# A single-token attention and MLP block: wq's load split into 16 and 112 rows

## The chip, the cores and the metric

The kernel runs on one core of one Trainium2 chip. Each core has five engines: TensorE (PE, matmuls and weight loads), VectorE (DVE), ScalarE (ACT), GpSimd (POOL) and SyncE (SP), and here SP issues nearly all of the loads. 16 DMA engines move the bytes from HBM to SBUF, the memory with 128 partitions from which the engines compute. The metric is the device time of one execution in microseconds; the time before is the median of three runs.

## The reference: what is computed

One token x of 512 values goes through a pre-norm block. Attention reads a cache of 32768 keys and values for each of 32 heads of width 128, and an MLP with a mish activation follows:

```python
q = (layernorm(x) @ wq) per head                 # wq 512 x 4096
p = softmax(q . k_cache * 128**-0.5)             # k_cache 32 x 32768 x 128, bf16
h = x + (p @ v_cache) @ wo                       # v_cache as k_cache, wo 4096 x 512
z = layernorm(h) @ w1 + b1                       # w1 512 x 1376
out = h + (z * tanh(softplus(z))) @ w2           # w2 1376 x 512
```

Each head has 8.39 MB of keys and as much of values. With one query there is one use for each byte that is loaded.

## The kernel before

SBUF holds a ring of six slots of 32 KB a partition (L354, `ring`). Two pairs of slots take the keys of even and odd heads in turn, one pair takes values; the weights lie in the same slots before and after (`HOMES`, L470). wq, 4 MB, is put into the first slot of the value pair: 128 partitions, 32 KB in each. Row p of the load holds rows 4p to 4p+3 of the matrix, so that it is one contiguous run of 32 KB in HBM.

`order` (L456 to L459) is the order in which SP issues loads: wq, the keys of head 0, and then for each head the next keys and the values before; at the end wo, the last values and the MLP's weights. wq itself is issued ahead of the Block that holds the engines' programs (L882). The SP program then starts with the two loads of the bias b1 (L563 and L564, behind a wait for GpSimd's zeroing of their tile), and goes on to the keys (L590). `start` (L550) issues a load on SP that raises a semaphore by 16 when it has landed. The keys of head 0 are cut into three loads and those of head 1 into two; all other key loads but the last are whole. The first values wait for wq's slot to be free (`freed_by`, L497).

Meanwhile x is loaded on ACT's queue (L601), turned by PE, and normalized (L623 to L639) into xnT. PE then makes all queries at once (L642 to L648): 128 matmuls, each with a 128 x 128 block of wq as weights, the first of which waits for xnT and for wq's semaphore. `ready_wait` (L484) gives that semaphore: `ready` of the slot, at 16 times the number of the fill, and wq is that slot's first fill. The last of these matmuls frees wq's slot.

For each head PE turns the keys, 128 x 128 at a time (L690), VectorE copies the turned keys out of PSUM (L696), and PE multiplies them with the query (L666). The softmax follows (L730 to L753), and PE multiplies the values with the weights (L717). PE's program is a loop over heads, as is VectorE's. The end is the projection by wo, the second layernorm, and the MLP (L788 to L872).

Of the kernel before, what the change touches and what calls it, by code (L numbers as in the profile page):

```python
# [291 lines left out]
def bass_sequential_preLN__mha_block_cached__dense_activation_mish__decode_kernel(  # L292
    nc: bass.Bass,
    A_x: bass.AP,
    A_k_cache: bass.AP,
    A_v_cache: bass.AP,
    A_wq: bass.AP,
    A_wo: bass.AP,
    B_x: bass.AP,
    B_w1: bass.AP,  # L300
    B_b1: bass.AP,
    B_w2: bass.AP,
    out: bass.AP,
):
    build_kernel(nc, A_x, A_k_cache, A_v_cache, A_wq, A_wo, B_w1, B_b1, B_w2, out)


def build_kernel(nc, A_x, A_k_cache, A_v_cache, A_wq, A_wo, B_w1, B_b1, B_w2, out):
# [6 lines left out]
    KC = D // 128  # L315
# [26 lines left out]
    def sb(shape, dt, name):  # L342
        cm = nc.sbuf_tensor(name, shape, dt)
        t = cm.__enter__()
        allocs.append(cm)
        return t.ap()
# [7 lines left out]
    ring = sb([128, NS, SLOT], BF16, "ring")  # L354
# [53 lines left out]
    sem = nc.alloc_semaphore  # L408
# [3 lines left out]
    ready = [sem(f"ready{i}") for i in range(NS)]  # L412
    sems["keys_in"] = (ready[0], ready[HALVES])
    s_x = sem("s_x")
    s_b1 = sem("s_b1")
    s_out = sem("s_out")
    WQ, WO, WL = ("wq",), ("wo",), ("wl",)
# [54 lines left out]
    def slot_of(what):  # L472
        if what in HOMES:
            return HOMES[what]
        if what[0] in ("w1", "w2"):
            return HOMES[WL]
        return V_HOME if what[0] == "v" else what[1] % 2 * HALVES
# [6 lines left out]
    def ready_wait(what):  # L484
        if what == WL:
            return (s_wl, 16)
        return (ready[slot_of(what)], 16 * fills[what])

    def free_name(what):
        return "free" + "_".join(map(str, what))  # L490
# [50 lines left out]
    def program(S):  # L541
# [13 lines left out]
        for what in order:  # L555
# [13 lines left out]
            elif what[0] == "w1":  # L569
                k = what[1]  # L570
                start(w1_v[:, k, :], B_w1[k * 128:(k + 1) * 128, :], w1_sems[k])
            elif what[0] == "w2":
                n = what[1]
# [6 lines left out]
            else:  # L580
                kind, h = what
# [14 lines left out]
              waits=["fin"])  # L596
# [45 lines left out]
        for h in range(H):  # L642
            for kc in range(KC):
                last = h == H - 1 and kc == KC - 1
                S.step(PE, lambda h=h, kc=kc: t_.matmul(Q_REG[:, h:h + 1], wq_v[:, kc, h * Dh:(h + 1) * Dh],  # L645
                                                         xnT[:, 0, kc:kc + 1], start=(kc == 0), stop=(kc == KC - 1)),
                       name=(["q", free_name(("wq",))] if last else None),
                       waits=(["xn0", ready_wait(("wq",))] if h == 0 and kc == 0 else ()))  # L648
        S.step(DVE, lambda: v.tensor_copy(qT[:, 0:H], Q_REG), name="qT", waits=["q"])  # L649
        S.step(DVE, lambda: v.tensor_copy(qcur[:, :], qT[:, 0:1]), name="qc0", waits=["qT", "qTz", "oTz"], kind="qc")  # L650

# [227 lines left out]
    log = {}  # L879
    counted = _Sched(nc, False, events, sems, log)  # L880
    program(counted)
    nc.sync.dma_start(ring[:, slot_of(WQ), :], A_wq.rearrange("(p k) n -> p (k n)", k=KC)).then_inc(ready[slot_of(WQ)], 16)  # L882
    with nc.Block() as block:
        for eng_name, attr in ((POOL, "gpsimd"), (SP, "sync"), (DVE, "vector"), (ACT, "scalar"), (PE, "tensor")):
            emitter = _Sched(nc, True, events, sems, log, only=eng_name)

            def _run(eng, emitter=emitter):
                program(emitter)
            getattr(block, attr)(_run)
            assert emitter.cnt == counted.cnt  # L890
# [31 lines left out]
```

## Time and profile before

| | |
|---|---|
| three runs | 1275.12, 1275.36, 1275.61 us; median 1275.36 |
| span of the profiled execution | 1273.1 us (its own device time isn't listed beside it) |
| PE busy | 1019.9 us, 80% |
| DVE busy | 718.2 us, 56% |
| bytes moved | 548.22 MB, mean 431 GB/s |
| mean granted TensorE clock | 0.766 |
| issue of wq | starts at 0.75 us, takes 0.39 us |

The span goes from the first to the last instruction of one execution. A busy share is an average over the whole span, and PE's includes time in which it works at a lower granted clock. The DMA share of a window is the mean busy share of the 16 DMA engines; a packet's bytes and time are booked where it starts, so that in short windows the share can exceed 1. A row of waits gives the engine and line that waited, on what, and how long in total, how often, and the longest.

### The profile page before, as it was taken

To read this page: it belongs to the slowest core of one execution; us is meant where nothing else is said; L and a number is where in the kernel's file an instruction comes from. 1 tells how busy PE (TensorE), PEld (TensorE's weight loads), DVE (VectorE), ACT (ScalarE), POOL (GpSimd) and SP (SyncE) were. 2 spreads that over 40 slices of the span, in tenths; PEclk is the share of its full clock that TensorE was granted. 3 is DMA by queue.
4 is the path that set the end of the run, shared out by engine and by line. 5 is a ranking of instruction groups with operands and counts; after the bars stand their busy time and mean duration, and the time that the engine had idled before them with its cause. 6 is when DMAs were issued, how large, how long until landed. Compare 5 with 4: busy or idle time off the path is not lost.

```text
span 1273.1 us, 54451 instructions
## 1 busy us (share of the span) xinstructions
PE 1019.9 (80%) x25046; PEld 993.3 (78%) x25047; DVE 718.2 (56%) x1257; ACT 20.6 (2%) x71; POOL 0.9 (0%) x7
## 2 busy tenths in 40 slices
PE   4789877779777789777798777797777897777996
PEld 4789877779777779777788777797777887777994
DVE  3656664456654456644566544566545666444661
ACT  0000000000000000000000000000000000000000
POOL 0000000000000000000000000000000000000000
PEclk9778877678877778776788777788767887777885
DMA  9999999999999999999999999999999999999998
GB/s 406 442 417 438 432 439 432 432 434 430 432 441 428 437 434 428 432 439 432 434 434 430 430 439 434 430 434 434 428 434 441 428 437 432 430 432 439 427 427 360
DMA packets 12214, 548.22 MB, mean 431 GB/s; under 512 B 1348, under 2 KB 1454, under 8 KB 2862
## 3 DMA queue, kind: packets, MB, share of 16 engines
q1 hardware_dynamic: 12204, 548.09, 99.7%
q8 instruction: 8, 0.13, 0.0%
q10 hardware_dynamic: 2, 0.00, 0.0%
HBM read 548.09 MB, written 0.00 MB: 431 GB/s over the span
## 4 chain that ended last, share of the span: by engine, by line
DMA 54%; DVE 23%; PE 19%; issue 2%; SPq 2%; POOL 0%; POOLq 0%
DMA ring<-in_A_k_cache_dram 51%; DVE ering L696 23%; PE ops L717 9%; PE tps L690 7%; DMA ring<-in_A_v_cache_dram 2%; SPq L551 2%; PE sps L666 1%; DMA ring<-in_B_w_dram 1%; PE hlp L741 1%; PE hlp L736 1%; PE hlp L751 0%; PE tps L867 0%; DVE pmax L730 0%; DVE perm L872 0%; DVE gmax L738 0%
## 5 line engine op out<-in xcount | busy, mean ns | idle before, releaser
L690 PE MATMUL tps<-identb,ring 128*128 128x128 bf16 x8192 | 671.7, 233 | 208.8 <-DMA ring<-in_A_k_cache_dram 203.2
L696 DVE COPY ering<-tps 128x1024 bf16<-128x1024 bf16 x1024 | 669.7, 691 | 261.6 <-PE tps L690 261.1
L690 PEld LDWEIGHTS tps<-identb,ring 128*128 x8192 | 525.4, 105 | 211.6 <-issue 211.6
L666 PE MATMUL sps<-qcur,ering 128*128 128x1 bf16 x8192 | 343.7, 164 | 7.3 <-DVE ering L696 6.6
L666 PEld LDWEIGHTS sps<-qcur,ering 128*128 128x128 bf16 x8192 | 309.4, 97 | 10.1 <-DVE ering L696 9.4
L717 PEld LDWEIGHTS ops<-pbuf,ring 128*128 128x128 bf16 x8192 | 226.4, 103 | 23.3 <-issue 15.1
L717 PE MATMUL ops<-pbuf,ring 128*128 128x1 bf16 x8192 | 231.3, 165 | 10.6 <-DMA ring<-in_A_v_cache_dram 7.2
L725 DVE TENSOR_TENSOR oT<-ops,rtotc 128x1 f32 x31 | 5.0, 161 | 110.6 <-PE ops L717 110.6
L738 DVE TENSOR_REDUCE gmax<-hlp 1x1 f32<-1x128 f32 x32 | 8.9, 279 | 64.5 <-PE hlp L736 64.5
L743 DVE TENSOR_SCALAR nbias<-hlp 128x1 f32<-128x1 f32 x32 | 5.1, 158 | 63.5 <-PE hlp L741 63.5
L746 ACT ACTIVATE pbuf<-sps,nbias 128x256 bf16<-128x256 f32 x32 | 15.2, 474 | 1219.7 <-PE ops L717 1166.8
L730 DVE TENSOR_REDUCE pmax<-sps 128x1 f32<-128x256 f32 x32 | 13.6, 424 | 14.3 <-PE sps L666 14.3
L736 PE MATMUL hlp<-ident,pmax 128*1 128x128 f32 x64 | 17.1, 363 | 2.5 <-issue 2.5
L741 PE MATMUL hlp<-gmax,onesmat 1*128 1x1 f32 x64 | 18.5, 356 | 0.4 <-DVE gmax L738 0.4
L741 PEld LDWEIGHTS hlp<-gmax,onesmat 1*128 1x128 f32 x64 | 15.8, 304 | 1.3 <-DVE gmax L738 0.9
L751 PE MATMUL hlp<-esum,onesmat 128*128 128x1 f32 x64 | 12.1, 259 | 4.7 <-issue 0.6
L751 PEld LDWEIGHTS hlp<-esum,onesmat 128*128 128x128 f32 x64 | 9.8, 191 | 7.1 <-issue 7.1
L645 PE MATMUL hlp<-xnT,ring 128*128 128x1 bf16 x128 | 3.6, 165 | 9.2 <-DMA ring<-in_A_wq_dram 9.2
L645 PEld LDWEIGHTS hlp<-xnT,ring 128*128 128x128 bf16 x128 | 3.5, 104 | 9.3 <-issue 9.3
L725 DVE TENSOR_TENSOR oL<-ops,rtotc 128x1 bf16<-128x1 f32 x1 | 0.2, 161 | 12.4 <-PE ops L717 12.4
L649 DVE CAST qT<-hlp 128x32 bf16<-128x32 f32 x1 | 0.2, 192 | 11.5 <-PE hlp L645 11.5
L746 ACT ACTIVATION_READ_ACCUMULATOR pbuf<-sps,nbias 128x1 f32 x32 | 6.2, 193 | 0.0
(82 smaller groups left out, 45.5 us busy)
## 6 DMA issues: line engine op xcount, KB each, us to landing
ring<-in_A_k_cache_dram SPq DMA_DIRECT2D x3, 4096.0 KB, 40.0
ring<-in_A_v_cache_dram SPq DMA_DIRECT2D x3, 4096.0 KB, 16.0
ring<-in_A_k_cache_dram SPq DMA_DIRECT2D x3, 2048.0 KB, 30.9
ring<-in_A_k_cache_dram SPq DMA_DIRECT2D x1, 6144.0 KB, 45.2
ring<-in_A_wq_dram SPq DMA_DIRECT2D x1, 4096.0 KB, 12.3
ring<-in_A_wo_dram SPq DMA_DIRECT2D x1, 4096.0 KB, 35.1
ring<-in_A_v_cache_dram SPq DMA_DIRECT2D x1, 2048.0 KB, 16.1
ring<-in_B_w_dram SPq DMA_DIRECT2D x4, 344.0 KB, 20.5
```

The source lines that it names most:

```text
L551: S.dma(SP, lambda: sp.dma_start(dst, src).then_inc(s, 16))
L645: S.step(PE, lambda h=h, kc=kc: t_.matmul(Q_REG[:, h:h + 1], wq_v[:, kc, h * Dh:(h + 1) * Dh], xnT[:, 0, kc:kc + 1], start=(kc == 0), stop ...
L666: S.step(PE, lambda r=r: t_.matmul(S_ps[:, col0 + r:col0 + r + 1], ering[:, bg % NE, r, :], qcur[:, :], start=True, stop=True), name=(name ...
L690: S.step(PE, lambda r=r, at=at: t_.matmul(tb[:, r * 128:(r + 1) * 128], key_tile(S, at), identb[:, :], is_transpose=True, start=True, stop ...
L696: S.step(DVE, lambda: v.tensor_copy(ering[:, bg % NE, :, :].rearrange("p r d -> p (r d)"), tb[:, :]), name=f"ev{bg}", waits=[f"trb{bg}"], ...
L717: S.step(PE, lambda r=r: t_.matmul(o_ps[:, 0:1], vt[:, r, :], pbuf[:, r:r + 1], start=(r == 0), stop=(r == SCOLS - 1)), name=(names or Non ...
L730: S.step(DVE, lambda: v.tensor_reduce(pmax[:, :], S_ps[:, 0:SCOLS], AXX, ALU.max), name=f"pmax{h}", waits=[f"qkh{h}"], kind="pmax")
L736: S.step(PE, lambda: t_.matmul(A_REG, pmax[:, :], ident[:, :], start=True, stop=True), name=f"A{h}", waits=[f"pmax{h}", "ident", f"rcp{h - ...
L738: S.step(DVE, lambda: v.tensor_reduce(gmax[:, :], A_REG, AXX, ALU.max), name=f"gmax{h}", waits=[f"A{h}"], kind="gmax")
L741: S.step(PE, lambda: t_.matmul(B_REG, onesm[0:1, :], gmax[:, :], start=True, stop=True), name=f"B{h}", waits=[f"gmax{h}", "consts0"] + ([] ...
L746: S.step(ACT, lambda: a.activation(pbuf[:, :], S_ps[:, 0:SCOLS], ACTF.Exp, bias=nb[:, :], scale=SC, accum_out=esum[:, :]), name=f"exp{h}", ...
L751: S.step(PE, lambda: t_.matmul(C_REG, onesm[:, :], esum[:, :], start=True, stop=True), name=f"C{h}", waits=[f"exp{h}"], kind="C")
```

## The change

The load of wq becomes two. The first has the first 16 rows of the load, to partitions 0 to 15, with a semaphore of its own; the second has the other 112 rows, to partitions 16 to 127, and raises the semaphore that the whole load raised. Both are issued by SP ahead of the Block. The first projection matmul waits for both. (A row here is a partition's 32 KB, four rows of the matrix.)

```diff
+    s_wq0 = sem("s_wq0")
...
-                       waits=(["xn0", ready_wait(("wq",))] if h == 0 and kc == 0 else ()))
+                       waits=(["xn0", (s_wq0, 16), ready_wait(("wq",))] if h == 0 and kc == 0 else ()))
...
-    nc.sync.dma_start(ring[:, slot_of(WQ), :], A_wq.rearrange("(p k) n -> p (k n)", k=KC)).then_inc(ready[slot_of(WQ)], 16)
+    wq_rows = A_wq.rearrange("(p k) n -> p (k n)", k=KC)
+    nc.sync.dma_start(ring[0:16, slot_of(WQ), :], wq_rows[0:16, :]).then_inc(s_wq0, 16)
+    nc.sync.dma_start(ring[16:128, slot_of(WQ), :], wq_rows[16:128, :]).then_inc(ready[slot_of(WQ)], 16)
```

## The prediction

> **What bounds the kernel now.** I read the profile's page first, then who waited for whom, then the DMA issues, and last the first 20 us of the timeline, where the change lies. From the page come the span and the DMA queue's totals:
>
> ```profile
> span 1273.1 us, 54451 instructions
> q1 hardware_dynamic: 12204, 548.09, 99.7%
> ```
>
> The one queue that carries the loads keeps the 16 DMA engines busy for 99.7% of the span. So the kernel is a stream of 548 MB, with some work at its two ends. The rows by window show how even the stream is, and where it starts (columns: PE, PEld, DVE, ACT and POOL busy, PE clock, DMA share, GB/s):
>
> ```profile
> 1.50:1.75 0.25, 0.00 (x0) 0.00 (x0) 0.25 (x2) 0.25 (x1) 0.00 (x0) 1.00 0.01 4
> 1.75:2.00 0.25, 0.00 (x0) 0.00 (x0) 0.22 (x3) 0.25 (x1) 0.00 (x0) 1.00 5.38 1442
> 31.40:1200.00 1168.60, 948.27 (x23346) 927.56 (x23343) 680.25 (x1163) 16.96 (x60) 0.00 (x0) 0.77 1.00 434
> ```
>
> Nothing moves before 1.75 us. (Bytes are booked where a packet starts, hence the 1442.) From 31 to 1200 us the rate is 434 GB/s with the engines always busy: 27.1 GB/s for each of the 16. The waits say that the other engines follow the stream:
>
> ```profile
> PE tps L690 <- DMA ring<-in_A_k_cache_dram: 203.2, 30, 7.8
> PE hlp L645 <- DMA ring<-in_A_wq_dram: 9.2, 1, 9.2
> SPq L551 <- PE ops L717: 1163.1, 33, 38.7
> ```
>
> PE sits 203 us waiting for keys, some 7 us a head. SP, which issues the loads, waits for PE to free the value slots, but that wait is covered. A head's values are 8.39 MB, 19.3 us at 434 GB/s, and they land this long after their issue:
>
> ```profile
> ring<-in_A_v_cache_dram SPq DMA_DIRECT2D x30, 26.1
> ```
>
> So 26.1 - 19.3 = 6.8 us of other loads still stand in the queue when a value load is issued; the engines don't run dry. It follows that time lost by the DMA engines in the first load isn't made up later: the slowest engine's loss goes through to the end, one for one. The other way round, later work on PE at the start costs nothing unless it starves the queue.
>
> **The change, part by part.** Everything it touches stands in the first 17 us:
>
> ```profile
> 0.75 0.39 SPq L882 DMA_DIRECT2D ring<-in_A_wq_dram  x1
> 1.34 0.63 SPq L551 DMA_DIRECT2D b1r<-in_B_b_dram  x2
> 2.01 2.38 SPq L551 DMA_DIRECT2D ring<-in_A_k_cache_dram  x5
> 4.93 0.29 DVE L638 TENSOR_SCALAR xnT<-lnx,lns 128x4 bf16<-128x4 f32 x1 [0.60 <-ACT lns L636]
> 13.13 3.55 PE L645 MATMUL hlp<-xnT,ring 128*128 128x1 bf16 x128 [9.25 <-DMA ring<-in_A_wq_dram]
> 16.71 0.33 SPq L551 DMA_DIRECT2D ring<-in_A_v_cache_dram  x1
> ```
>
> One more issue on SP. The issue of wq takes 0.39 us, that of values 0.33, that of the two bias rows 0.63/2 = 0.32. So SP is occupied 0.3 to 0.4 us more, and the bias loads and the five key loads behind it are issued that much later. The key loads are not due until wq has been moved, at about 12 us, and the first is issued at 2.0 us: 10 us of cover, cost nothing. Without that cover it would cost 0.4 us. The other 112 rows are issued at about 1.1 us, while the first 16 haven't started moving. If Block's entry held the other engines back by 0.4 us too, that would be covered as well: the normalized x is ready at 4.93 + 0.29 = 5.2 us and wq at 13.1.
>
> A semaphore and a wait on PE. The first projection matmul waits for one semaphore more. Behind it on PE are the 128 matmuls of L645, which need the other 112 rows anyway; those land later, so the new wait is over first. Between nothing and one more row of the small PE work there, 0.17 us (3.55 us for 128 matmuls is 0.03 each, and each lasts 0.165), and not on the DMA path: zero.
>
> The start. The first bytes could move earlier, since an issue of 16 rows may be over before one of 128. The gain lies between nothing and the whole issue, 0.39 us. The issue of b1r's few rows, 0.32, is the nearest row: I take 0.39 - 0.32 = 0.1 us of gain, and the rest of it goes into the range.
>
> The moving of the 16 rows. This is the term that decides. The old load is 128 rows of 32 KB, all 128 partitions at once:
>
> ```profile
> q1 hardware_dynamic: 128, 4.19, 98.8%
> ring<-in_A_wq_dram SPq DMA_DIRECT2D x1, 4096.0 KB, 12.3
> ```
>
> The first row is from the DMA view of the window 1.5 to 12.0 us: 128 packets in the load queue, one a row, eight an engine. At 27.1 GB/s a row of 32768 B takes 1.21 us, eight take 9.7. Are the 16 rows still spread over the 16 engines? A load of few rows stands in the trace: b1r's 2.5 KB are five rows of 512 B, right behind wq. The DMA view of 12.13 to 12.30 us, then that of 12.13 to 12.65:
>
> ```profile
> DMA packets 18, 0.10 MB, mean 586 GB/s; under 512 B 10, under 2 KB 12, under 8 KB 12
> DMA packets 42, 0.25 MB, mean 478 GB/s; under 512 B 22, under 2 KB 27, under 8 KB 27
> ```
>
> Packets of 512 B to 2 KB are 12 - 10 = 2 by 12.30 and 27 - 22 = 5 by 12.65. Five rows on one engine would have followed each other at once; they are spread over the half microsecond in which the 16 engines finish wq. So rows are dealt to different engines: 16 rows go one to each engine, and 112 go seven to each. The engines are as evenly loaded as before. What isn't even is where they write: all 16 write into partitions 0 to 15, an eighth of SBUF's partitions. No load of this trace with long rows does that.
>
> Bounds. If SBUF takes bytes at any partition at any rate, the cost is nothing. If it takes them only so fast at any one place, then by the steady row the place fed by one engine, eight partitions, need not be able to take more than 27.1 GB/s; call that a group. Let the 16 rows lie in g of the 16 groups. Then 16/g rows queue for each, 16/g x 1.21 us, while the groups that hold none of them stand idle, with all of their eight rows still to come. The loss is thus 19.4/g us: 9.7 for g = 2 (eight neighbours a group), 4.85 for g = 4, 2.4 for g = 8. Between 2.4 and 9.7 I take the middle by ratio, 4.85. [...]
>
> The other 112 rows, if there are groups. Seven rows to each engine in order, 16 engines on groups that their seven-row stretches straddle: when two meet, each is halved, and neither can step aside. From below nothing; from above, say, an engine meets another in half of its rows, 3.5 x 1.21 = 4.2 us. I take the half, 2.1.
>
> Sum: -0.1 (start) + 0 + 0 + 4.85 + 2.1 = +6.85, taken as +6.9 us. The profile's own execution goes from a span of 1273.1 to 1280.0. The median of the runs, 1275.36, lies 2.26 us above that span, which I leave as it is: 1282.3 us. [...]
>
> What the delay does behind it: the projection ends at 16.7 + 6.9 = 23.6 us, and the first values are issued then. The queue at that point still holds the keys of two heads, 16.8 MB or 38.7 us behind wq, so it doesn't run dry.
>
> **The rivals.** No limit by place: the engines are the limit, and the change does nothing beyond the start's -0.4 to 0 and +0.1 of noise: 1275.0 to 1275.5, likeliest 1275.3. For it speaks the last load of the weights, 96 rows of 1 KB to 96 partitions. First its row among the issues, and its packets, the only ones over 512 B left in the window 1269.56 to 1269.84; then the rates of an earlier stretch, in which loads to all partitions are moved, and of this one:
>
> ```profile
> ring<-in_B_w_dram SPq DMA_DIRECT2D x1, 96.0 KB, 9.8
> DMA packets 31, 0.03 MB, mean 92 GB/s; under 512 B 6, under 2 KB 31, under 8 KB 31
> 1267.00:1267.50 0.50, 0.50 (x10) 0.50 (x7) 0.21 (x1) 0.00 (x0) 0.00 (x0) 0.50 1.06 389
> 1269.56:1269.66 0.10, 0.10 (x12) 0.10 (x12) 0.00 (x0) 0.00 (x0) 0.00 (x0) 0.50 0.41 143
> ```
>
> Per busy engine that is 389/(1.06 x 16) = 22.9 GB/s before and 143/(0.41 x 16) = 21.8 with the partial load: hardly a loss, with smaller packets. Against it: only some 6.6 engines are busy, with 1 KB rows, spread over 96 partitions and not 16, so two seldom meet for long. The rival decides where a group can take at least what four engines bring, 108 GB/s. This is the case that ends on the other side, not slower.
>
> Faster by more than 2.55 us (0.2%): it would need the start. Before 1.75 us nothing moves. The first load's 4.19 MB, 9.7 us at full rate, takes from 1.75 to about 12.1, some 0.65 us over. Both together are 2.4 us: even with all of it gone, it isn't reached.
>
> Dealt worse: if the second load's rows go round the engines in turn, 16 neighbouring rows are again written at one time, seven times over, and at g = 4 the loss is eight times 4.85 less the 9.7 of before, +29 us: 1304. If the small load sat on four engines alone, those would have four rows each and then seven more, 11 in place of 8: +3.6 us, 1279, with no need of a limit by place. The bias rows speak against the second; for the first there is nothing but the neighbourhood of the rows.
>
> **How the numbers follow.** A limit by place with +2.6 to +9.7 us: 0.48. No limit: 0.39. Dealt worse: 0.10, half of it beyond the range. Faster: 0.03. Slower by over 0.2% is 0.48 + 0.10 = 0.58, within 0.2% is 0.39, faster 0.03; 0.2% is about what a measurement of this kernel can tell from no change. The range has to take in the no-limit case, whose weight is too large to leave out, and the upper bound of 9.7: 1274.9 to 1285.1, which leaves out about one in ten. The likeliest case by itself is 1278 to 1285.1, with 1282.3 as its value.
>
> **What would show it.** Right: wq's second load lands at about 19 to 20 us after the start of the span in place of 13.1; the rate in the window from 1.75 to 6.5 us is near 110 GB/s for the first 512 KB and below 434 up to 18 us; L645 begins some 7 us later; the stretch from 31 to 1200 us is unchanged at 434. If the rate is low for the first 5 us alone, the second term was wrong and the time is near 1280. Wrong: L645 starts within 0.5 us of 13.1, and DMA stays at its rate from 3 us on; then no place limits the engines. Wrong in another way: the first window is slow, and the end doesn't move; then some slack in the stream was overlooked.

## The result and the profile after

The change makes the kernel slower by 9.2 us: 1284.39 us (1283.69 to 1284.50, five runs) beside 1275.18 (1275.12 to 1275.61, five runs), a ratio of 1.007 with a 95% interval of 1.0059 to 1.0081. The forecast was 1282.3, between 1274.9 and 1285.1. The profiled execution is the fastest of the five, 1283.69 us, with a span 8.8 us longer than that of before; the spans of the other four are 1282.5 and 1282.6.

First the page's totals and the rows of waits that answer to those of before:

```profile
span 1281.9 us, 54452 instructions
q1 hardware_dynamic: 12220, 548.09, 99.7%
...
PE tps L691 <- DMA ring<-in_A_k_cache_dram: 205.2, 30, 7.7
PE hlp L646 <- DMA ring<-in_A_wq_dram: 18.5, 1, 18.5
SPq L552 <- PE ops L718: 1165.5, 33, 38.7
```

Same bytes, same busy share of the DMA engines, nearly the same waits behind. Only the wait for wq has grown, from 9.2 to 18.5 us. (The change adds one line, so L645 is now L646.) The start of the timeline shows the new issues and the projection:

```profile
0.75 0.40 SPq L884 DMA_DIRECT2D ring<-in_A_wq_dram  x1
1.20 0.40 SPq L885 DMA_DIRECT2D ring<-in_A_wq_dram  x1
1.73 0.58 SPq L552 DMA_DIRECT2D b1r<-in_B_b_dram  x2
2.36 2.26 SPq L552 DMA_DIRECT2D ring<-in_A_k_cache_dram  x5
22.40 3.55 PE L646 MATMUL hlp<-xnT,ring 128*128 128x1 bf16 x128 [18.51 <-DMA ring<-in_A_wq_dram]
25.98 0.33 SPq L552 DMA_DIRECT2D ring<-in_A_v_cache_dram  x1
```

The projection starts at 22.40 us in place of 13.13, 9.3 later. The DMA issues give the size of each load and the time from issue to landing; the windows give DMA share and GB/s as their last two columns:

```profile
ring<-in_A_wq_dram SPq DMA_DIRECT2D x1, 3584.0 KB, 21.1
ring<-in_A_wq_dram SPq DMA_DIRECT2D x1, 512.0 KB, 6.6
```

```profile
1.75:2.00 0.25, 0.00 (x0) 0.00 (x0) 0.22 (x3) 0.25 (x1) 0.00 (x0) 1.00 10.89 1573
2.00:12.00 10.00, 0.98 (x10) 0.82 (x10) 1.46 (x9) 1.07 (x3) 0.00 (x0) 1.00 0.78 170
12.00:21.00 9.00, 0.00 (x0) 0.00 (x0) 0.00 (x0) 0.00 (x0) 0.00 (x0) 1.00 1.01 259
40.00:1200.00 1160.00, 938.38 (x23169) 917.62 (x23167) 672.47 (x1151) 16.95 (x60) 0.00 (x0) 0.77 1.00 434
```

The small load lands at 0.75 + 6.6 = 7.35 us, the large one at 1.20 + 21.1 = 22.3. From 2 to 21 us the engines move some 210 GB/s, and from 40 us on 434 as before. The same window of both kernels in the DMA view, 0 to 21 us, tells where the time went. Before:

```profile
DMA packets 363, 8.28 MB, mean 394 GB/s; under 512 B 40, under 2 KB 46, under 8 KB 46
...
q1 hardware_dynamic: 360, 8.26, 94.6%
```

After:

```profile
DMA packets 186, 4.43 MB, mean 211 GB/s; under 512 B 38, under 2 KB 44, under 8 KB 44
...
q1 hardware_dynamic: 184, 4.43, 93.2%
```

By 21 us the changed kernel has started 3.85 MB fewer, which at 434 GB/s is 8.9 us: the whole difference of the spans. And yet the engines are as busy, 93.2% beside 94.6%. So the busy share counts time in which little is moved: 211 GB/s beside 394 at nearly the same share. The share alone doesn't show the loss, share and GB/s together do.

### The profile page after: what moved, and what is told of

Its sections match the earlier page's. It is cut to its first block, busy times and chain, and to the rows that moved or that the text cites. A ratio compares the mean times of both kernels' runs of the same rounds, so it can differ in the third digit from the quotient of the medians.

```text
span 1281.9 us, 54452 instructions
## 1 busy us (share of the span) xinstructions
PE 1015.8 (79%) x25046; PEld 988.9 (77%) x25047; DVE 717.6 (56%) x1257; ACT 20.6 (2%) x71; POOL 0.9 (0%) x7
## 4 chain that ended last, share of the span: by engine, by line
DMA 55%; DVE 23%; PE 18%; issue 2%; SPq 2%
DMA ring<-in_A_k_cache_dram 52%; DVE ering L697 23%; PE ops L718 9%; PE tps L691 6%; DMA ring<-in_A_v_cache_dram 2%; SPq L552 2%; PE sps L667 1%; DMA ring<-in_B_w_dram 1%; PE hlp L742 1%; PE hlp L737 1%; PE hlp L752 0%; PE tps L868 0%; DVE pmax L731 0%; SPq L885 0%; SPq L884 0%
## 5 line engine op out<-in xcount | busy, mean ns | idle before, releaser
L742 PE MATMUL hlp<-gmax,onesmat 1*128 1x1 f32 x64 | 18.5, 356 | 0.4 <-DVE gmax L739 0.4
L646 PE MATMUL hlp<-xnT,ring 128*128 128x1 bf16 x128 | 3.6, 165 | 18.5 <-DMA ring<-in_A_wq_dram 18.5
L646 PEld LDWEIGHTS hlp<-xnT,ring 128*128 128x128 bf16 x128 | 3.5, 104 | 18.6 <-issue 18.6
L737 PEld LDWEIGHTS hlp<-ident,pmax 128*1 128x1 f32 x64 | 2.7, 81 | 5.3 <-issue 4.8
## 6 DMA issues: line engine op xcount, KB each, us to landing
ring<-in_A_wq_dram SPq DMA_DIRECT2D x1, 3584.0 KB, 21.1
```

The costliest lines, as they stand in the source:

```text
L737: S.step(PE, lambda: t_.matmul(A_REG, pmax[:, :], ident[:, :], start=True, stop=True), name=f"A{h}", waits=[f"pmax{h}", "ident", f"rcp{h - ...
L742: S.step(PE, lambda: t_.matmul(B_REG, onesm[0:1, :], gmax[:, :], start=True, stop=True), name=f"B{h}", waits=[f"gmax{h}", "consts0"] + ([] ...
```

## The experiments

The theory: SBUF takes bytes at any one place only as fast as one engine brings them, and 16 neighbouring rows, then 112 rows dealt seven to an engine, let several engines meet at one place while others stand empty. Its rivals: two loads cost something as such; reading neighbouring rows disturbs HBM; or the rows of a short load sit on few engines. The first four kernels share 24 runs of the kernel before on their chip, median 1275.11 us; the last four share seven, median 1275.07.

**Two loads, cut by columns.** Same sizes, same semaphores, all partitions in both:

```diff
-    nc.sync.dma_start(ring[0:16, slot_of(WQ), :], wq_rows[0:16, :]).then_inc(s_wq0, 16)
-    nc.sync.dma_start(ring[16:128, slot_of(WQ), :], wq_rows[16:128, :]).then_inc(ready[slot_of(WQ)], 16)
+    nc.sync.dma_start(ring[:, slot_of(WQ), 0:2048], wq_rows[:, 0:2048]).then_inc(s_wq0, 16)
+    nc.sync.dma_start(ring[:, slot_of(WQ), 2048:SLOT], wq_rows[:, 2048:SLOT]).then_inc(ready[slot_of(WQ)], 16)
```

> wq is two loads as in the change, of the same 0.5 and 3.5 MB and with the same two semaphores, but cut by columns: both go to all 128 partitions (4 KB and 28 KB a partition). Limit by place in SBUF: no place is fed by more than one engine, so the time is that of before, 1275.2, within 0.5 us. A cost of the second load as such (its issue, its semaphore, a pause between loads): the +9.2 us of the change again, 1284.4. Two loads that disturb each other only where the rows are few: as the first.

Measured: 1275.01 us, ratio 1.000 (0.999 to 1.001). The two loads' rows among its DMA issues:

```profile
ring<-in_A_wq_dram SPq DMA_DIRECT2D x1, 3584.0 KB, 11.7
ring<-in_A_wq_dram SPq DMA_DIRECT2D x1, 512.0 KB, 3.6
```

The same 512 KB land 3.6 us after their issue in place of 6.6, and the same 3.5 MB 11.7 after theirs in place of 21.1. So a second load, its issue, its semaphore and the added wait cost nothing that shows here; the span of the profiled execution, 1273.1 us, is that of before.

**The 16 rows alone.** The first load goes to the neighbour slot, which is empty until the values come, and the whole of wq follows as before the change:

```diff
+    nc.sync.dma_start(ring[0:16, slot_of(WQ) + 1, :], wq_rows[0:16, :]).then_inc(s_wq0, 16)
+    nc.sync.dma_start(ring[:, slot_of(WQ), :], wq_rows).then_inc(ready[slot_of(WQ)], 16)
```

> The first load of the change alone: 16 rows of wq to partitions 0 to 15 of the empty neighbour slot, then the whole wq to all 128 partitions as before. So 0.5 MB is loaded twice, which is +1.2 us by bytes. Limit by place with four places for these partitions: the 16 rows take 4.85 us in which the other places stand idle, and the whole of wq comes after: +4.85 us, 1280.0, and the small load lands at about 7.3 us as in the change. Cost of two loads as such: +9 to +10. No limit: +1.2, 1276.4. If the small load sits on four engines: also +4.85, which the next run tells apart.

Measured: 1278.92 us, +3.8 us, ratio 1.003 (1.0019 to 1.0042). This kernel moves 0.5 MB more than the changed one and is 5.5 us faster.

**The same rows to other partitions.** Then the same partitions from other rows:

```diff
+    nc.sync.dma_start(ring[0:128:8, slot_of(WQ) + 1, :], wq_rows[0:16, :]).then_inc(s_wq0, 16)
...
+    nc.sync.dma_start(ring[0:16, slot_of(WQ) + 1, :], wq_rows[0:128:8, :]).then_inc(s_wq0, 16)
```

> As the run before, from the same 16 neighbouring rows of HBM, but to every eighth partition of the slot. [...] A limit on the side of HBM (16 neighbouring rows read at one time): as the run before, +4.85. 16 rows that sit on four engines: as the run before, +4.85. No limit: +1.2.

> The reverse of the run before: every eighth row of wq in HBM, to the neighbouring partitions 0 to 15 of the empty slot, then the whole wq. Limit by place in SBUF: as with neighbouring rows, +4.85 us. A limit on the side of HBM: less, down to +1.2. The 16 rows on four engines: +4.85.

Measured: 1277.32 us, +2.2, ratio 1.0017 (1.0007 to 1.0026), with the rows spread over SBUF; 1279.36, +4.3, ratio 1.0033 (1.0021 to 1.0046), with the rows spread over HBM and neighbours in SBUF. The small load's row in the three kernels, neighbours in both, spread in SBUF, spread in HBM:

```profile
ring<-in_A_wq_dram SPq DMA_DIRECT2D x1, 512.0 KB, 6.6
```

```profile
ring<-in_A_wq_dram SPq DMA_DIRECT2D x1, 512.0 KB, 5.1
```

```profile
ring<-in_A_wq_dram SPq DMA_DIRECT2D x1, 512.0 KB, 7.2
```

The time follows the partitions: neighbours in SBUF are slow whichever rows of HBM they come from, 6.6 and 7.2 us beside 5.1. Spreading the rows over HBM wins nothing, and costs 0.4 us more than neighbours in both (1279.36 beside 1278.92); why wasn't tried. In the spread kernel the issue itself took 0.64 us and not 0.40, so that its load could start 0.2 us later at the least, and that is part of the 5.1 us. Nor are few engines at work. In the window 1.5 to 2.5 us the packets are x's two and 16 rows of 32 KB, and this line is the same in the kernel before and in the changed one:

```profile
DMA packets 18, 0.53 MB, mean 525 GB/s; under 512 B 1, under 2 KB 2, under 8 KB 2
```

Before, 128 rows wait to be moved, and yet only 16 start in this time, so an engine doesn't take up several rows at once. The changed kernel's 16 rows start in it too and are thus on 16 engines. What differs is how long they take. The 0.75 us in which they start, before and then after the change:

```profile
1.75:2.50 0.75, 0.25 (x8) 0.26 (x8) 0.47 (x4) 0.75 (x1) 0.00 (x0) 1.00 2.46 699
1.75:2.50 0.75, 0.25 (x8) 0.26 (x8) 0.47 (x4) 0.75 (x1) 0.00 (x0) 1.00 4.86 699
```

A packet's whole time is booked where it starts. So the shares, means over 16 engines, give the mean time of one of the 16 rows: 2.46 x 0.75 = 1.8 us before, and 4.86 x 0.75 = 3.6 us with all 16 going to partitions 0 to 15.

**The 112 rows alone**, ahead of the whole wq:

```diff
+    nc.sync.dma_start(ring[16:128, slot_of(WQ) + 1, :], wq_rows[16:128, :]).then_inc(s_wq0, 16)
+    nc.sync.dma_start(ring[:, slot_of(WQ), :], wq_rows).then_inc(ready[slot_of(WQ)], 16)
```

> The second load of the change by itself, with nothing ahead of it: rows 16 to 127 to the neighbour slot, then the whole wq as before. 3.67 MB are loaded twice, +8.5 us by bytes. [...]

Measured: 1289.63 us, +14.6, ratio 1.0113 (1.0096 to 1.013). Its row, and a window:

```profile
ring<-in_A_wq_dram SPq DMA_DIRECT2D x1, 3584.0 KB, 17.6
```

```profile
2.00:12.00 10.00, 0.98 (x10) 0.81 (x10) 1.46 (x9) 1.07 (x3) 0.00 (x0) 1.00 0.99 256
```

Of the 14.6 us, 8.5 are bytes. The other 6.1 are lost with no small load ahead at all: the engines stand at a share of 0.99 and move 256 GB/s, so that a row takes 2.0 us in place of 1.21. 112 rows over 16 engines, though evenly loaded, aren't a full-rate load here.

**Eight loads of 16 rows**, neighbours in one kernel and eight apart in the other, with the same number of issues and the same sizes (the projection waits for `s_wq0` at 112):

```diff
+    for i in range(8):
+        nc.sync.dma_start(ring[16 * i:16 * i + 16, slot_of(WQ), :], wq_rows[16 * i:16 * i + 16, :]).then_inc(
+            s_wq0 if i < 7 else ready[slot_of(WQ)], 16)
...
+        nc.sync.dma_start(ring[i:128:8, slot_of(WQ), :], wq_rows[i:128:8, :]).then_inc(
+            s_wq0 if i < 7 else ready[slot_of(WQ)], 16)
```

> wq as eight loads of 16 neighbouring rows each, to partitions 0 to 15, 16 to 31, and so on. [...] No limit, or a limit in HBM that is met by reading all rows in order: under +1. A cost of each load as such: seven times 9.2.

> The same number of loads of the same size, each of 16 rows eight apart, in HBM and in SBUF. [...] A cost of each load as such, or a few engines that get all rows of a load: the same as the run before.

Measured: 1301.33 us with neighbours, +26.3, ratio 1.0207 (1.019 to 1.0224); 1285.45 with rows eight apart, +10.4, ratio 1.0082 (1.0066 to 1.0099). Bytes are booked where a row starts, so the windows shown hold whole rounds, six of 16 rows each (3.15 MB), first with neighbours and then with rows apart:

```profile
9.65:37.05 27.40, 0.00 (x0) 0.00 (x0) 0.00 (x0) 0.00 (x0) 0.00 (x0) 1.00 1.01 115
```

```profile
6.64:21.80 15.16, 0.00 (x0) 0.00 (x0) 0.00 (x0) 0.00 (x0) 0.00 (x0) 1.00 1.01 208
```

115 GB/s is 26% of 434, and 208 is 48%, with all 16 engines busy: a row takes 4.6 us with neighbours and 2.5 with rows apart, in place of 1.21. With equal numbers of loads and rows the layout sets the rate here. In this pair the rows of HBM change along with the partitions; that the partitions decide is what the 16 rows alone have shown.

**Two halves.**

```diff
+    nc.sync.dma_start(ring[0:64, slot_of(WQ), :], wq_rows[0:64, :]).then_inc(s_wq0, 16)
+    nc.sync.dma_start(ring[64:128, slot_of(WQ), :], wq_rows[64:128, :]).then_inc(ready[slot_of(WQ)], 16)
```

> wq as two loads of 64 rows. If the places were eight neighbouring partitions each, four neighbouring rows to an engine would meet at most in pairs and eight places would stand idle: half of the rate. [...] If only few rows are slow and 64 are enough to fill all places: +0.

Measured: 1285.58 us, +10.5, ratio 1.0083 (1.0066 to 1.0099), a slowing as by half of the rate, and 0.8 us more than the 9.7 that wq's 4.19 MB would lose by that (9.7 us at 434 GB/s, twice that at half). The evenest cut by rows is a little worse than the change. Six rounds of 16 rows in this kernel:

```profile
6.55:21.75 15.20, 0.00 (x0) 0.00 (x0) 0.00 (x0) 0.00 (x0) 0.00 (x0) 1.00 1.00 207
```

That is about half of 434, as with rows eight apart.

None of these is faster than the kernel before; the one that costs nothing, the cut by columns, gains nothing either.

## Why the prediction was right, and where its sizes were off

What bounds the kernel: right. The loss arises in the first 21 us, the stream from 40 us on has the same 434 GB/s, and the projection's delay of 9.3 us comes out at the end as 9.2.

The issue and the wait: right, nothing. The keys' first issue moved from 2.01 to 2.36 us, hidden as said, and the cut by columns has a second load with its semaphore and wait at a median 0.1 us below that of before, with an interval of 1.3 us to either side.

The start: no gain, where 0.1 us was taken. The nearest row, the issue of b1r, was the wrong neighbour: the issue of 16 rows takes 0.40 us, that of 128 took 0.39, and in both kernels nothing but x moves before 1.75 us.

The 16 rows: that the loss follows the partitions is shown (6.6 and 7.2 us to landing at neighbours, 5.1 spread), and the size was 4.85 beside 3.8 measured. The choice of four places between two and eight, an estimate, fits: the small load lands 6.6 us after its issue in both kernels that have it, and with two places it would have been 4.85 us more. Of the missing 1.0 us, 0.3 would be the rate of a place: taken at four places, the 115 GB/s of the eight loads of neighbours are 28.7 GB/s at each, a little more than the 27.1 of an engine, and so 4.6 us a row and not 4.85. The rest fits the start: the first rows of before take 1.8 us and not 1.21, some 0.6 us longer, while the 16 rows of the change take 3.6 and not 4.6 or more. That rows held up at a place hide the slow start wasn't tried by itself.

The 112 rows: the term that was mis-sized. "An engine meets another in half of its rows, 3.5 x 1.21 = 4.2 us. I take the half, 2.1." The change's 9.2 less the 3.8 of the first load leaves 5.4, above even the upper bound. The load by itself loses 6.1 us. By the estimate of 16 places with eight partitions each, 1.2 of these would be the fullest place, which has eight rows where an engine has seven, and 4.9 would be left for engines that meet. The bound took for granted that an engine meets another in half of its rows at the most. That engines meet is an inference from the loss with evenly loaded engines (256 GB/s at a share of 0.99) and from the rates of 115 and 208 GB/s; how often, and which rows each engine has, no run shows. That 9.2 still lies within the stated range is in part luck: its top, 9.7, is the first term with two places, a case that didn't occur. Four places and the second term's upper bound come to 4.85 + 4.2 - 0.1 = 8.95.

Which partitions share a place no run shows. 16 neighbours get 115 GB/s, about a quarter of 434, which would make four neighbouring partitions a place; 64 neighbours would then be 16 places, but get 207 GB/s, about half.

The rival of no limit had 0.39 on the strength of the 96-row load at the end, which runs at 21.8 GB/s a busy engine. That row was read rightly and weighed too high: it has only 6.6 engines at work, with six rows of 1 KB each. What takes up such short meetings wasn't tried. The two cases of "dealt worse" didn't occur. Of those the round-robin deal is what the eight loads of neighbours do by hand: +26.3, for which +29 was worked out.

Of the signs named ahead, the rate below 434 to 18 us and the unchanged stream came as said. The "near 110 GB/s for the first 512 KB" didn't: 16 rows side by side at 3.6 us each are some 144 GB/s, the same 1.0 us of the first term. The second load landed at 22.3 us and not at 19 to 20, the same miss of the second term.

## What to carry to other kernels

A load that covers part of the partitions wasn't just smaller here: wq cut by columns, with all 128 partitions in each part, took 1275.01 us beside 1275.11 whole, and cut by rows it cost 9.2 to 26.3 us. So try the cut by columns first for a load that sits on the critical stream. Where a stream of loads bounds the kernel, a few microseconds lost at its start can reach the end whole: here the projection's 9.3 us came out as 9.2, with PE busy for 79% of the span. Read DMA share and GB/s together: the eight loads of neighbours had a share of 1.01 at 115 GB/s, the steady stream 1.00 at 434.

## What else the runs showed of the hardware

The time of an issue on SP doesn't follow the number of rows in these runs: 0.39 us for 128 rows, 0.40 for 16 and 0.40 for 112 neighbours. A row in every eighth partition took 0.64, and the first issue of 64 rows 0.58:

```profile
0.74 0.58 SPq L884 DMA_DIRECT2D ring<-in_A_wq_dram  x1
```

The change has its first rows under way from 1.75 us on, and so has the whole load before (1573 and 1442 GB/s from 1.75 to 2.00 us). So an early small load has no head start to win here.
